# Linear attention and two mixers on one core: theta tiles loaded first, low parts and the first batch's products on VectorE, weight pieces at other units

## The chip, the cores and the metric

One core of a Trainium2 chip runs the whole program in one launch. The metric is the device time of an execution in microseconds. Three executions of the kernel before took 1168.22, 1164.98 and 1165.29 us; their median, 1165.29, is the time before. Engines are named as in the profile: PE (TensorE's matmuls; PEld its weight loads), DVE (VectorE), ACT (ScalarE), POOL (GpSimd), SP (SyncE, which here only issues transfers).

## What is computed

Eight batches of 576 tokens by 512 features go through three blocks. The reference, cut:

```python
kv = einsum('bhsd,bhse->bhde', k, v)      # attention without softmax, 8 heads of 64
x  = (q @ kv) / rms(q @ kv) * g_norm      # per head
theta = x @ w_theta
y = w_tok_r @ (x * cos(theta)) + w_tok_i @ (x * sin(theta))
u = x + y
x = u + relu(u @ w_ch)                    # first mixer
u = x + (relu(x.T @ w_tok1) @ w_tok2).T   # second mixer, over tokens: 576 -> 256 -> 576
out = u + relu(u @ w_ch1) @ w_ch2         # second mixer, over features: 512 -> 1536 -> 512
```

The weights come as float64 and are read as pairs of int32 words, from which the chip builds fp32 values.

## The kernel before, in words

**Products.** Every large product runs as three fp16 products, high by high, high by low and low by high (mm3, L82 to L84). So each operand needs a high part (an ACT copy to fp16) and a low part (value minus high part). "Decoding" a weight tile (L120 to L130) is one ACT instruction (L123) and three DVE instructions (L128, L129, L130). In `weight` (L132) the theta weights then take one ACT and one DVE instruction (L155, L157); all others take two ACT instructions (a scale, L150; the high part, L151) and one on POOL for the low part (L153).

**Units.** The work of a batch is cut into units: `attend` (normalised heads x, tiles a0 to a4), `rotate` (theta product pt, cosine and sine, multiply by x, high part zh and low part zl; r0 to r4), `mix` (M, products py over tokens, then uh and ul), `channel` (C, products pr, then xs high and low, and a DMA transpose of xs into xt, L464, after every second C unit), `token1` (H, products ph from xt, split at L71 and L72), `token2` (T, products pu; the result goes to a DRAM tile u2d). The two digits of M, C, H, T are the column chunk or part and the feature tile. In the first batch x reaches its transposed form by PE transposes (px, L322), later by DMA transposes (L330). `rotate_last` (L373) makes the last 64 tokens of both rotations as one tile zt (L399), which a DMA transpose (L400) puts into zh.

**Order.** `go` starts a unit after it has moved each pending unit on by one step (a yield). Lists of units (MIX, CHANNEL, STEADY) and a table, BESIDE, say what is started beside which unit: "a2", "r1" for the next batch, "l" for its loads, "n0" for the batch after that, "w" for a piece from the list `extra`. In the steady batches a piece is `stash` (L191): two transfers of 256 KB each on SP's queue at its start (wa_r or wb_r), seven steps later the decode (L128 to L130 on 128x512), sums on POOL (L213 to L216), the high part on ACT (L218), the low part on DVE (L220) and two stores. 24 such pieces prepare the weights of the last block and are spread over batches 1 to 6, five in a full batch. The program order that results goes through a scheduler, which may move an instruction ahead of others where its own simulation says so; urgent() puts the residual steps of `mix` and `channel` first.

**Transfers.** SP issues all loads of k, v, q and weights and all DMA transposes in one queue, in program order. POOL issues the stores to DRAM.

**Last block.** `mlp` (L545) handles 8 pairs of 288-column halves with seven products per 2x2 block. The first part forms pa, pb, pc (L555 on), the second na, nb, nc with the results added on DVE in `add` (L622). In program order the second part runs product 6 for both tiles, then 5, 7, 3, 4.

Of the kernel before, what the change touches and what calls it, by code (L numbers as in the profile page):

```python
# [28 lines left out]
def attn_mixer_kernel(  # L29
# [32 lines left out]
    def bank(name):  # L62
        return ps.tile([P, 512], F32, tag="ps", name=name)
# [68 lines left out]
    def weight(pool, w, src, part, n, hi, lo, scale, name, raw=None):  # L132

        val = pool.tile([P, S // 2], F32, tag="val", name=f"{name}v")[:part, :n] if pool is not stg else \
            pool.tile([P, n], F32, tag="val", name=f"{name}v")[:part]
        if w.dtype == F32:
            load(val, src)
            yield
        else:
            if raw is None:  # L140
                raw = pool.tile([P, 4, P, 2] if pool is not stg else [P, n, 2], I32, tag="raw", name=f"{name}r")
                if pool is not stg:
                    raw = raw.rearrange("p a n w -> p (a n) w")
                raw = raw[:part, :n]
                load(raw.rearrange("p n w -> p (n w)"), src)
            yield
            yield from decode(val, raw)
        if w is not w_theta:

            nc.scalar.activation(val, val, AF.Copy, scale=scale)  # L150
            nc.scalar.activation(hi, val, AF.Copy)  # L151
            yield
            nc.gpsimd.tensor_tensor(lo, val, hi, ALU.subtract)  # L153
            return
        nc.scalar.activation(hi, val, AF.Copy, scale=scale)  # L155
        yield
        nc.vector.scalar_tensor_tensor(lo, val, scale, hi, ALU.mult, ALU.subtract)  # L157
# [185 lines left out]
    def rotate(o, r):  # L343

        b = o.b
        if r == 0:
            prepare(o)
        zh, zl, x, xt = o.zh, o.zl, o.x[r], o.xt[r]
        if r == NR:
            yield from rotate_last(o, xt)  # L350
            return
        pt = bank(f"pt{b}{r}")
        mm3(pt, [(xt[:, 0, kk, :], xt[:, 1, kk, :], wth[:, kk, :], wtl[:, kk, :]) for kk in range(KD)])

        cs = fp.tile([P, 2, DM], F32, tag="cs", name=f"cs{b}{r}", bufs=2)
        f, sn = cs[:, 0], cs[:, 1]
        mul = nc.gpsimd if b == 0 else nc.vector
        yield
        nc.scalar.activation(f, pt, AF.Copy, bias=MAGIC)
        nc.vector.scalar_tensor_tensor(f, f, MAGIC, pt, ALU.subtract, ALU.subtract)  # L360
        yield
        nc.scalar.activation(sn, f, AF.Sin, scale=-RAD)
        nc.scalar.activation(f, f, AF.Abs)
        nc.scalar.activation(f, f, AF.Sin, bias=hpi, scale=-RAD)
        yield
        mul.tensor_tensor(cs, cs, x.unsqueeze(1).to_broadcast([P, 2, DM]), ALU.mult)
        yield
        at = slice(r, r + NR + 1, NR)
        nc.scalar.activation(zh[:, at, :], cs, AF.Copy)
        yield  # L370
        nc.vector.tensor_tensor(zl[:, at, :], cs, zh[:, at, :], ALU.subtract)  # L371
# [173 lines left out]
    def mlp(i, ck, following):  # L545
# [67 lines left out]
        def narrow(p, m, g, acc, first):  # L613
            ws, xs = PRODUCTS[p]
            h = hidden[g]
            part = (wb[0][:, g, m, ws], wb[1][:, g, m, ws], h.hi[:, xs], h.lo[:, xs])
            mm3(acc, [part], first=first and g == 0, last=g == KH - 1, skip_group_check=True)
# [30 lines left out]
            add(pb[m], m, 0, 0, True)  # L648
        nxt = next(following, None)

        def run(p, acc, first):
            for m in range(MH):
                if acc[m] is None:
                    acc[m] = bank(f"nc{i}{m}")[:, :NC]
                for g in range(KH):
                    narrow(p, m, g, acc[m], first)

        run(6, pa, False)
        for m in range(MH):
            add(pa[m], m, 0, 1)  # L660
        next(following, None)
        run(5, pc, True)
        for m in range(MH):
            add(pc[m], m, 1, 1)
        next(following, None)
        run(7, pa, False)
        for m in range(MH):
            add(pa[m], m, 1, 1, True)
        next(following, None)
        run(3, pc, False)  # L670
        for m in range(MH):
            add(pc[m], m, 0, 1, True)
        run(4, pa, False)
        for m in range(MH):
            add(pa[m], m, 1, 0, True)
        return nxt

# [28 lines left out]

    tk, cp, first = [], [], iter(())
    for j in range(KD):
        if j == 1:
            o = load_heads(0)  # L710
        go(weight_tile(stg, w_theta, wt, j, DM, ST / (2.0 * math.pi), "wt"))
    for part in range(2):
# [23 lines left out]
    def run(units, o, nxt, after, beside):  # L736
# [23 lines left out]
    TOKENS1 = ["K00", "H00", "H01", "K10", "H10", "H11"]  # L760
    STEADY = MIX[:6] + CHANNEL[:2] + MIX[6:] + CHANNEL[2:4] + ["K00"] + CHANNEL[4:] + TOKENS1[1:] + TOKEN2
    BESIDE = {
        "M00": "a2", "M01": "a3", "M02": "a4 l", "M03": "r0", "M10": "w", "M11": "r1", "M12": "r2", "M13": "w",
        "C03": "r4", "C11": "w", "H01": "r3", "H11": "n0 w", "T01": "n1", "T10": "w",
    }
    for b in range(B):
        loaded.clear()
# [23 lines left out]
        elif b == 1:  # L791
# [2 lines left out]
            run(MIX[4:6] + CHANNEL[:1], o, nxt, None, {"M10": "a2", "M11": "a3", "C00": "a4 l"})  # L794
            after = loaded[0]
            run(STEADY[STEADY.index("C01"):], o, nxt, after, {
                "C01": "r0", "M12": "r1", "M13": "r2", "C03": "r4", "C11": "w", "H01": "r3", "H11": "n0 w", "T01": "n1", "T10": "w",
            })
        elif b + 2 < B:
            at = STEADY.index("M02") + 1  # L800
# [81 lines left out]
```

## Time and profile before

| | |
|---|---|
| median of three executions | 1165.29 us |
| profiled execution, its own time | 1169.86 us |
| its span in the trace | 1168.1 us |
| PE busy | 1084.4 us, 93% |
| DVE busy | 823.4 us, 70% |
| ACT busy | 570.5 us, 49% |
| POOL busy | 266.8 us, 23%, nothing after about 600 us |
| mean granted clock of PE | 0.975 of full |

The span is what the profiler saw between first and last instruction; the execution's own time lies 1.8 us above it. The first batch takes the first 97 us and shares PE with the loading and decoding of the weights; batches 1 to 7 run until about 640 us, each some 73 to 78 us long; the last block fills the rest. "PEclk" is the granted clock as a share of 2.4 GHz: 1.00 is that level, and a stretch that reads between 0.5 and 1 was partly at 1.2 GHz.

### The profile page before, as it was taken

The numbers are of one execution on the slowest core, as the hardware profiler recorded it, in microseconds if no ns is written. First come the engines' busy times: TensorE is split into PE (matmuls) and PEld (weight loads), VectorE is DVE, ScalarE is ACT, GpSimd is POOL, SyncE is SP. The second block draws the span as 40 slices with busy tenths as digits, with TensorE's granted clock in tenths as the row PEclk, the third lists the DMA queues.
The fourth block names the chain that finished last, engine by engine and source line by source line (L and its number), as shares of the span: only waits on it lengthen the run. The fifth ranks groups of instructions, "written<-read, shape, count | busy, mean of one in ns | idle before, by whom it ended". The sixth has DMA issues, their size and how long they took to land.

```text
span 1168.1 us, 21694 instructions
## 1 busy us (share of the span) xinstructions
PE 1084.4 (93%) x8884; PEld 820.2 (70%) x8884; DVE 823.4 (70%) x1449; ACT 570.5 (49%) x980; POOL 266.8 (23%) x316
## 2 busy tenths in 40 slices
PE   4768889899998998999999999999999999999998
PEld 4456666576675875766677777777777777777776
DVE  3987857688787887787846395758567494848583
ACT  3766634646355454554724273626445362626261
POOL 2774134072542734625400000000000000000000
PEclk9879989999999998999999999999999999999999
DMA  9616446674766646745283801111010202010101
GB/s 319 210 69 142 104 124 147 167 185 107 215 148 173 184 124 176 184 127 145 59 246 78 308 2 42 41 36 47 23 60 11 72 11 72 1 57 26 37 6 41
DMA packets 146082, 126.34 MB, mean 108 GB/s; under 512 B 93184, under 2 KB 121984, under 8 KB 145984
## 3 DMA queue, kind: packets, MB, share of 16 engines
q1 hardware_dynamic: 140608, 104.53, 33.2%
q0 software_dynamic: 5376, 20.45, 5.0%
q8 instruction: 69, 1.13, 0.4%
q14 instruction: 29, 0.24, 0.1%
HBM read 74.29 MB, written 29.88 MB: 89 GB/s over the span
## 4 chain that ended last, share of the span: by engine, by line
PE 35%; DVE 28%; DMA 15%; ACT 10%; POOL 7%; issue 4%; SPq 1%; ACTq 0%; POOLq 0%; DVEq 0%
DMA xt<-xs 7%; PE na L82 3%; PE na L84 3%; PE na L83 3%; DVE gl L563 3%; DMA c<-u2d 2%; DVE gl L611 2%; POOL ri L308 2%; PE pa L82 2%; ACT gh L562 2%; PE pa L83 2%; PE pa L84 2%; DMA u2d<-R 1%; DVE zl L371 1%; PE nc L84 1%
## 5 line engine op out<-in xcount | busy, mean ns | idle before, releaser
L82 PE MATMUL py<-wmh,zh 128*128 128x256 f16 (+1 forms) x576 | 166.4, 289 | 9.4 <-DMA zh<-zt 6.0
L83 PE MATMUL py<-wml,zh 128*128 128x256 f16 (+1 forms) x576 | 166.3, 289 | 0.0
L84 PE MATMUL py<-wmh,zl 128*128 128x320 f16 (+1 forms) x512 | 146.1, 288 | 2.3 <-DVE zl L371 2.3
L82 PE MATMUL na<-gh,wbh 128*128 128x288 f16 x384 | 107.2, 287 | 9.8 <-DVE c L622 9.8
L83 PE MATMUL na<-gl,wbh 128*128 128x288 f16 x384 | 109.6, 288 | 0.0
L82 PE MATMUL pa<-o,wah 128*128 128x288 f16 x384 | 108.8, 286 | 0.9 <-DVE pre L605 0.9
L84 PE MATMUL na<-gh,wbl 128*128 128x288 f16 x384 | 109.5, 288 | 0.0
L83 PE MATMUL pa<-o,wah 128*128 128x288 f16 x384 | 109.5, 286 | 0.0
L84 PE MATMUL pa<-o,wal 128*128 128x288 f16 x384 | 108.7, 286 | 0.0
L622 DVE SCALAR_TENSOR_TENSOR c<-na,c 128x288 f32<-128x288 f32 x64 | 28.5, 455 | 81.2 <-PE na L84 81.2
L83 PEld LDWEIGHTS <-wbh 128*128 128x128 f16 x672 | 65.9, 98 | 27.6 <-issue 11.0
L563 DVE TENSOR_TENSOR gl<-sum,gh 128x1152 f16<-128x1152 f32 x48 | 65.1, 1356 | 24.3 <-ACT gh L562 23.5
L83 PEld LDWEIGHTS <-wah 128*128 128x128 f16 x672 | 65.8, 98 | 18.1 <-issue 1.3
L84 PEld LDWEIGHTS <-wbl 128*128 128x128 f16 x672 | 65.9, 98 | 16.8
L82 PEld LDWEIGHTS <-wbh 128*128 128x128 f16 x672 | 65.9, 98 | 16.8
L82 PEld LDWEIGHTS <-wah 128*128 128x128 f16 x672 | 65.8, 98 | 16.7
L84 PEld LDWEIGHTS <-wal 128*128 128x128 f16 x672 | 65.8, 98 | 16.6
L83 PE MATMUL pr<-ul,wch 128*128 128x256 f16 (+1 forms) x256 | 73.1, 286 | 3.4 <-DVE ul L430 3.4
L82 PEld LDWEIGHTS <-zh 128*128 128x128 f16 x576 | 57.1, 99 | 26.0 <-DMA zh<-zt 6.6
L82 PE MATMUL pr<-uh,wch 128*128 128x256 f16 (+1 forms) x256 | 73.0, 286 | 1.1 <-ACT uh L427 1.1
L84 PE MATMUL pr<-uh,wcl 128*128 128x256 f16 (+1 forms) x256 | 73.1, 286 | 0.0
L308 POOL TENSOR_TENSOR ri<-ss,mhalf 128x8 f32<-128x8 f32 x40 | 69.2, 1731 | 2.0
(311 smaller groups left out, 2983.9 us busy)
## 6 DMA issues: line engine op xcount, KB each, us to landing
q<-in_q SPq DMA_DIRECT2D x8, 1152.0 KB, 5.9
c<-u2d SPq DMA_DIRECT2D x32, 288.0 KB, 4.4
out<-c SPq DMA_DIRECT2D x64, 144.0 KB, 1.8
k<-in_k SPq DMA_DIRECT2D x24, 256.0 KB, 5.7
v<-in_v SPq DMA_DIRECT2D x24, 256.0 KB, 6.0
wa_r<-in_w_ch SPq DMA_DIRECT2D x24, 256.0 KB, 4.4
wb_r<-in_w_ch SPq DMA_DIRECT2D x24, 256.0 KB, 4.6
wad<-wa POOLq DMA_DIRECT2D x24, 224.0 KB, 2.4
```

The lines of the kernel that those rows point to most:

```text
L82: nc.tensor.matmul(acc, ah, bh, start=first and i == 0, stop=False, **more)
L83: nc.tensor.matmul(acc, ah, bl, start=False, stop=False, **more)
L84: nc.tensor.matmul(acc, al, bh, start=False, stop=last and i == n - 1, **more)
L308: nc.gpsimd.tensor_tensor(ri, ss, mhalf, ALU.pow)
L371: nc.vector.tensor_tensor(zl[:, at, :], cs, zh[:, at, :], ALU.subtract)
L562: nc.scalar.activation(h.hi[:, 3:], h.s, AF.Copy)
L563: nc.vector.tensor_tensor(h.lo[:, 3:], h.s, h.hi[:, 3:], ALU.subtract)
L611: nc.vector.tensor_tensor(h.lo[:, :3], h.own, h.hi[:, :3], ALU.subtract)
L622: nc.vector.scalar_tensor_tensor(dst, acc, 1.0 / SW**2, dst, ALU.mult, ALU.add)
```

## The change

1. Tiles 0 to 2 of the theta weights are loaded ahead of the first batch's k, v and q; before, only tile 0 was.
2. In the first batch the multiplication of cosine and sine by x (four instructions of 128x1024, L366) runs on DVE, not POOL.
3. All weights take the path that theta took: 22 low parts (9 token tiles of 576 columns, 4 channel tiles, 9 for the second mixer) go from POOL to DVE, and 22 scale instructions on ACT (L150) go away, the scale being part of the other two.
4. Pieces "w" start at M02, C10, H01, T01 and T12 where they started at M10, M13, C11, H11 and T10; in batch 1 at C10, H01, T01, T12 for C11, H11, T10.
5. The second part of `mlp` is written tile by tile: 5 and 6 of tile 0, 5 and 6 of tile 1, 7 and 3 of tile 0, 7 and 3 of tile 1, then 4.

Line numbers of the changed kernel are 7 to 10 lower behind `weight` (L464 is L456, L460 is L452, L399 is L391).

```diff
@@ weight
             yield
             yield from decode(val, raw)
-        if w is not w_theta:
-
-            nc.scalar.activation(val, val, AF.Copy, scale=scale)
-            nc.scalar.activation(hi, val, AF.Copy)
-            yield
-            nc.gpsimd.tensor_tensor(lo, val, hi, ALU.subtract)
-            return
         nc.scalar.activation(hi, val, AF.Copy, scale=scale)
         yield
         nc.vector.scalar_tensor_tensor(lo, val, scale, hi, ALU.mult, ALU.subtract)
@@ rotate
-        mul = nc.gpsimd if b == 0 else nc.vector
...
-        mul.tensor_tensor(cs, cs, x.unsqueeze(1).to_broadcast([P, 2, DM]), ALU.mult)
+        nc.vector.tensor_tensor(cs, cs, x.unsqueeze(1).to_broadcast([P, 2, DM]), ALU.mult)
@@ mlp
-        def run(p, acc, first):
-            for m in range(MH):
-                if acc[m] is None:
-                    acc[m] = bank(f"nc{i}{m}")[:, :NC]
-                for g in range(KH):
-                    narrow(p, m, g, acc[m], first)
-
-        run(6, pa, False)
+        def run(p, m, acc, first):
+            if acc[m] is None:
+                acc[m] = bank(f"nc{i}{m}")[:, :NC]
+            for g in range(KH):
+                narrow(p, m, g, acc[m], first)
+
+
         for m in range(MH):
+            run(5, m, pc, True)
+            add(pc[m], m, 1, 1)
+            run(6, m, pa, False)
             add(pa[m], m, 0, 1)
-        next(following, None)
-        run(5, pc, True)
+            next(following, None)
         for m in range(MH):
-            add(pc[m], m, 1, 1)
-        next(following, None)
-        run(7, pa, False)
+            run(7, m, pa, False)
+            add(pa[m], m, 1, 1, True)
+            run(3, m, pc, False)
+            add(pc[m], m, 0, 1, True)
+            if m == 0:
+                next(following, None)
         for m in range(MH):
-            add(pa[m], m, 1, 1, True)
-        next(following, None)
-        run(3, pc, False)
-        for m in range(MH):
-            add(pc[m], m, 0, 1, True)
-        run(4, pa, False)
-        for m in range(MH):
+            run(4, m, pa, False)
             add(pa[m], m, 1, 0, True)
         return nxt
@@ theta tiles and the first heads
     for j in range(KD):
-        if j == 1:
+        if j == KD - 1:
             o = load_heads(0)
         go(weight_tile(stg, w_theta, wt, j, DM, ST / (2.0 * math.pi), "wt"))
@@ steady batches; the table of batch 1 loses C11, H11, T10 and gains C10, H01, T01, T12 likewise
     BESIDE = {
-        "M00": "a2", "M01": "a3", "M02": "a4 l", "M03": "r0", "M10": "w", "M11": "r1", "M12": "r2", "M13": "w",
-        "C03": "r4", "C11": "w", "H01": "r3", "H11": "n0 w", "T01": "n1", "T10": "w",
+        "M00": "a2", "M01": "a3", "M02": "a4 l w", "M03": "r0", "M11": "r1", "M12": "r2",
+        "C03": "r4", "C10": "w", "H01": "r3 w", "H11": "n0", "T01": "n1 w", "T12": "w",
     }
```

**SP's queue at the end of `channel` in a steady batch (the fourth).** xt<-xs of 8x128 ends chunk 0, the two of 10x128 are chunk 1, zh<-zt is the next batch's last rotated tile, wa_r are halves of a piece. Before, from the transpose that ends chunk 0:

```order
L464 DMA_TRANSPOSE xt_2834<-xs_2972 128x8x128
L249 DMA k_3091<-in_k 96x512
L249 DMA v_3093<-in_v 96x512
L400 DMA_TRANSPOSE zh_2711<-zt_3058 128x8x128
L464 DMA_TRANSPOSE xt_3095<-xs_3096 128x10x128
L116 DMA wa_r<-in_w_ch 128x2x256
L464 DMA_TRANSPOSE xt_3095<-xs_3145 128x10x128
L116 DMA wa_r<-in_w_ch 128x2x256 x3
L249 DMA k_3563<-in_k 128x512
```

and in the changed kernel:

```order
L456 DMA_TRANSPOSE xt_2829<-xs_2963 128x8x128
L242 DMA k_3082<-in_k 96x512
L242 DMA v_3084<-in_v 96x512
L116 DMA wa_r<-in_w_ch 128x2x256 x2
L392 DMA_TRANSPOSE zh_2714<-zt_3050 128x8x128
L456 DMA_TRANSPOSE xt_3086<-xs_3087 128x10x128
L456 DMA_TRANSPOSE xt_3086<-xs_3128 128x10x128
L116 DMA wa_r<-in_w_ch 128x2x256 x4
L242 DMA k_3552<-in_k 128x512
```

The piece half that stood between the two transposes of chunk 1 is gone from there; two halves now stand ahead of zh<-zt, and four instead of three follow behind the last transpose.

**DVE at the same place.** R<-pr adds a channel product to the residual, xs<-R are the low parts that the transpose takes, wa_s is the decode of a piece. Before:

```order
L128 TENSOR_SCALAR wa_s<-wa_s 128x512
L452 SCALAR_TENSOR_TENSOR R_1648<-pr_3113,R_1648 128x320
L129 SCALAR_TENSOR_TENSOR wa_s<-wa_r,wa_s 128x512
L399 TENSOR_TENSOR zt_3058<-cs_3057,zt_3058 128x512
L460 SCALAR_TENSOR_TENSOR xs_3096<-R_1648,xs_3096 128x256
L460 SCALAR_TENSOR_TENSOR xs_3096<-R_1648,xs_3096 128x64
L130 SCALAR_TENSOR_TENSOR wa_s<-wa_r,wa_s 128x512
L452 SCALAR_TENSOR_TENSOR R_1648<-pr_3146,R_1648 128x320
L452 SCALAR_TENSOR_TENSOR R_1648<-pr_3165,R_1648 128x320
L460 SCALAR_TENSOR_TENSOR xs_3145<-R_1648,xs_3145 128x256
L460 SCALAR_TENSOR_TENSOR xs_3145<-R_1648,xs_3145 128x64
L460 SCALAR_TENSOR_TENSOR xs_3145<-R_1648,xs_3145 128x256
```

and in the changed kernel:

```order
L391 TENSOR_TENSOR zt_3050<-cs_3049,zt_3050 128x512
L444 SCALAR_TENSOR_TENSOR R_1626<-pr_3113,R_1626 128x320
L444 SCALAR_TENSOR_TENSOR R_1626<-pr_3129,R_1626 128x320
L452 SCALAR_TENSOR_TENSOR xs_3087<-R_1626,xs_3087 128x256
L452 SCALAR_TENSOR_TENSOR xs_3087<-R_1626,xs_3087 128x64
L452 SCALAR_TENSOR_TENSOR xs_3128<-R_1626,xs_3128 128x256
L452 SCALAR_TENSOR_TENSOR xs_3128<-R_1626,xs_3128 128x64
L444 SCALAR_TENSOR_TENSOR R_1626<-pr_3147,R_1626 128x320
L452 SCALAR_TENSOR_TENSOR xs_3128<-R_1626,xs_3128 128x256
L452 SCALAR_TENSOR_TENSOR xs_3128<-R_1626,xs_3128 128x64
L128 TENSOR_SCALAR wa_s<-wa_s 128x512
L129 SCALAR_TENSOR_TENSOR wa_s<-wa_r,wa_s 128x512
```

The three decode instructions that stood among the last R and xs steps follow behind the last xs; so the last four xs are no longer behind L130.

**DVE at the joint of two pairs of the last block.** c<-na, c<-nb and c<-nc are the additions of `add`; o, own and gl belong to the next pair's first part. Before:

```order
L622 SCALAR_TENSOR_TENSOR c_6785<-nb_7814,c_6785 128x288
L542 SCALAR_TENSOR_TENSOR o_7925<-t_7926,o_7924 128x1152
L585 TENSOR_TENSOR own_8160<-pb_8153,m_8151 128x288
L622 SCALAR_TENSOR_TENSOR c_6785<-nb_7818,c_6785 128x288
L610 TENSOR_TENSOR sum_7873<-own_7753,sum_7873 128x288
L563 TENSOR_TENSOR gl_7869<-sum_7873,gh_7868 128x1152
L585 TENSOR_TENSOR own_8194<-pb_8187,m_8177 128x288
L589 TENSOR_TENSOR own_8160<-pc_8196,u_8185 128x288
L622 SCALAR_TENSOR_TENSOR c_6785<-na_7806,c_6785 128x288
L622 SCALAR_TENSOR_TENSOR c_6785<-na_7810,c_6785 128x288
L622 SCALAR_TENSOR_TENSOR c_6785<-nc_7977,c_6785 128x288
L622 SCALAR_TENSOR_TENSOR c_6785<-nc_7996,c_6785 128x288
```

and in the changed kernel:

```order
L614 SCALAR_TENSOR_TENSOR c_6763<-nb_7792,c_6763 128x288
L534 SCALAR_TENSOR_TENSOR o_7903<-t_7904,o_7902 128x1152
L577 TENSOR_TENSOR own_8138<-pb_8131,m_8129 128x288
L614 SCALAR_TENSOR_TENSOR c_6763<-nb_7796,c_6763 128x288
L602 TENSOR_TENSOR sum_7851<-own_7731,sum_7851 128x288
L555 TENSOR_TENSOR gl_7847<-sum_7851,gh_7846 128x1152
L577 TENSOR_TENSOR own_8172<-pb_8165,m_8155 128x288
L581 TENSOR_TENSOR own_8138<-pc_8174,u_8163 128x288
L614 SCALAR_TENSOR_TENSOR c_6763<-nc_7909,c_6763 128x288
L614 SCALAR_TENSOR_TENSOR c_6763<-na_7784,c_6763 128x288
L614 SCALAR_TENSOR_TENSOR c_6763<-nc_7956,c_6763 128x288
L614 SCALAR_TENSOR_TENSOR c_6763<-na_7788,c_6763 128x288
```

Up to the last own both kernels have the same rows; of the four additions behind it, nc and na now alternate. Apart from the last pair, PE's queue differs by the same alternation alone: in both kernels it issues 15 matmuls of na directly behind the pb products that open the next pair.

## Rows read from the trace of the kernel before

**Rows 1.** Page, part 1: busy us, share of the span, instructions.

```profile
PE 1084.4 (93%) x8884; PEld 820.2 (70%) x8884; DVE 823.4 (70%) x1449; ACT 570.5 (49%) x980; POOL 266.8 (23%) x316
```

**Rows 2.** PE's waits over the whole span: total us, times, longest.

```profile
PE na L82 <- DVE c L622: 9.8, 6, 2.0
```

**Rows 3.** PE's waits, 0 to 97.4 us (the first batch).

```profile
PE px L322 <- DVE x L314: 7.2, 4, 3.1
...
PE py L82 <- ACT zh L369: 3.4, 1, 3.4
PE py L82 <- DMA zh<-zt: 3.0, 1, 3.0
```

**Rows 4.** PE's waits, 225 to 560 us (the steady batches).

```profile
PE ph L480 <- DMA xt<-xs: 15.7, 6, 4.2
PE pr L83 <- DVE ul L430: 3.0, 4, 0.9
```

**Rows 5.** Windows of token product 1 (ph): stretch, length, busy (instructions), PEclk, DMA share, GB/s.

```profile
295.00:302.83 7.83, 3.61 (x16) 0.00 (x0) 0.00 (x0) 1.00 1.04 270
...
sum 29.69, PE 25.47 DVE 1.64 ACT 2.37; mean PE 5.09 DVE 0.33 ACT 0.47
```

**Rows 6.** SP timeline, 366 to 375 us: start, us, instruction.

```profile
369.82 0.68 SPq L116 DMA_DIRECT2D wa_r<-in_w_ch  x1
370.63 1.33 SPq L464 DMA_TRANSPOSE xt<-xs  x1
```

**Rows 7.** DVE timeline, 364.3 to 371.2 us: start, us, instruction.

```profile
364.98 0.43 DVE L128 TENSOR_SCALAR wa_s<-wa_s 128x512 int32<-128x512 int32 x1
...
365.72 0.68 DVE L129 SCALAR_TENSOR_TENSOR wa_s<-wa_r,wa_s 128x512 int32<-128x512 int32 x1
...
367.40 0.68 DVE L130 SCALAR_TENSOR_TENSOR wa_s<-wa_r,wa_s 128x512 int32<-128x512 int32 x1
...
369.02 1.55 DVE L460 SCALAR_TENSOR_TENSOR xs<-R,xs 128x256 f16<-128x256 f32 x4
```

**Rows 8.** Chain that ended last: start, us to landing.

```profile
370.63 5.03 DMA xt<-xs
```

**Rows 9.** One line's instructions: transposes of xs issued by L464.

```profile
DMA to landing us min/median/max: 3.0/3.5/9.2
```

**Rows 10.** DVE by line and form, 230 to 600 us: busy, mean ns, idle before.

```profile
L371 DVE TENSOR_TENSOR zl<-cs,zh 128x1024 f16<-128x1024 f32 x21 | 26.9, 1283 | 4.5 <-ACT zh L369 4.3
L366 DVE TENSOR_TENSOR cs<-cs,x 128x1024 f32<-128x1024 f32 x20 | 25.5, 1275 | 6.0 <-ACT cs L364 5.9
```

**Rows 11.** DVE by line and form, 20 to 97 us.

```profile
L371 DVE TENSOR_TENSOR zl<-cs,zh 128x1024 f16<-128x1024 f32 x4 | 7.6, 1908 | 3.5 <-ACT zh L369 3.4
...
L157 DVE SCALAR_TENSOR_TENSOR wtl<-wt_3v,wth 128x512 f16<-128x512 f32 x1 | 0.7, 678 | 0.0
```

**Rows 12.** POOL by line and form, 16 to 97 us.

```profile
L309 POOL TENSOR_TENSOR x<-ri,gb 128x512 f32<-128x512 f32 x9 | 12.0, 1336 | 0.3
L366 POOL TENSOR_TENSOR cs<-cs,x 128x1024 f32<-128x1024 f32 x4 | 9.9, 2480 | 0.0
...
L153 POOL TENSOR_TENSOR wml<-wm_8v,wmh 128x576 f16<-128x576 f32 x1 | 2.3, 2257 | 0.0
...
L153 POOL TENSOR_TENSOR wcl<-wc_1v,wch 128x512 f16<-128x512 f32 x1 | 1.1, 1146 | 0.0
```

**Rows 13.** POOL timeline, 49 to 62 us.

```profile
53.82 2.87 POOL L366 TENSOR_TENSOR cs<-cs,x 128x1024 f32<-128x1024 f32 x1
```

**Rows 14.** DVE timeline, 49 to 62 us.

```profile
54.40 2.62 DVE L128 TENSOR_SCALAR wm_5v<-wm_5v 128x576 int32<-128x576 int32 x1
...
60.80 0.45 DVE L128 TENSOR_SCALAR wm_6v<-wm_6v 128x576 int32<-128x576 int32 x1
```

**Rows 15.** Windows, all engines: PE, PEld, DVE, ACT, POOL busy, PEclk, DMA share, GB/s.

```profile
0.00:20.00 20.00, 7.66 (x89) 6.90 (x90) 2.94 (x5) 2.95 (x4) 1.29 (x10) 1.00 0.88 278
...
97.40:163.00 65.60, 58.51 (x485) 40.30 (x483) 47.90 (x100) 40.96 (x87) 13.87 (x14) 0.93 0.55 134
```

More of the change, by code (lines that the diff above doesn't have):

```diff
@@ L796, in attn_mixer_kernel @@
             run(STEADY[STEADY.index("C01"):], o, nxt, after, {
-                "C01": "r0", "M12": "r1", "M13": "r2", "C03": "r4", "C11": "w", "H01": "r3", "H11": "n0 w", "T01": "n1", "T10": "w",
+                "C01": "r0", "M12": "r1", "M13": "r2", "C03": "r4", "C10": "w", "H01": "r3 w", "H11": "n0", "T01": "n1 w", "T12": "w",
             })
```

## The prediction

> **What bounds the kernel now.** I read the page's busy times first: PE is busy 1084.4 us, 93% of the span [rows 1], so a change that leaves the products alone can only win what PE waits, and the half clock that follows some waits. The view of PE's waits then says where. In the last block the largest item is 9.8 us for the additions on DVE [rows 2]. In the first batch PE waits for x out of DVE (7.2), for a high part zh (3.4) and for the DMA transpose of the last rotated tile (3.0) [rows 3]. In the steady batches nearly all of it is one thing: token product 1 (ph) waits six times, 15.7 us in all, for the DMA transpose xt<-xs, and a channel product waits 3.0 us for low parts ul [rows 4]. Third, windows of ph alone show what the waits cost beyond themselves: its 16 matmuls take 3.61 us where PE kept its full clock, and five such groups together 25.47 us [rows 5], so 25.47 - 5 x 3.61 = 7.4 us go to half clock behind the wait.
>
> Why that transpose is late is read from the two queues ahead of it. On DVE the three decode instructions of a weight piece (0.43, 0.68, 0.68 us) stand among the last residual and xs steps; the last four xs start at 369.02 and take 1.55 us, to 370.57 [rows 7]; the transpose is issued at 370.63 [rows 6]. So DVE sets the issue. SP sends a 256 KB half piece at 369.82 [rows 6], which is over by then and delays no issue, but it is in flight when the transpose starts: that one lands after 5.03 us [rows 8], against a median of 3.5 [rows 9].
>
> **Steady batches, the pieces moved.** The order shows the decode behind the last xs and the half piece gone from between the two transposes. Issue comes 0.43 + 0.68 + 0.68 = 1.8 us earlier, and landing another 5.03 - 3.5 = 1.5 earlier if nothing large is in flight. The mean wait is 15.7 / 6 = 2.6 us. Bounds: 1.8 off each wait, less where a wait is shorter, some 9 us; at best all 15.7. I take 12, since two half pieces now stand ahead of all three transposes and part of the 1.5 will not come. Of the 7.4 us at half clock I take 5 (0 to 7.4): it hangs on waits going, not shrinking. Of the 3.0 for ul, 2 (0 to 3.0), as a piece no longer starts beside M10 and M13. Against it: a piece's decode, POOL sums, high and low parts now run beside H, T and the next M units, where DVE had no piece before. No row shows that wait; the nearest is ul's, 3.0 us in four, 0.75 each [rows 4]. One per batch over four full batches is +3 (0 to +6). Behind a delayed DVE the next to be late would be R<-pu, and behind it POOL's store of u2d, which nobody needs until the last block. The k and v loads behind the four half pieces on SP start later; PE has a whole batch until it reads them, so 0. Sum -12 - 5 - 2 + 3 = **-16**, from -26 to -3.
>
> **First batch.** Added to DVE ahead of zt: four multiplications at 1.275 us [rows 10] = 5.1, nine low parts of 576 columns at 0.678 [rows 11] x 576/512 = 0.76, so 6.9, and two of 512, 1.4. Together 13.4. What goes is contention. A decode instruction that started at 54.40 took 2.62 us, where the same one at 60.80 took 0.45 [rows 14]; POOL was multiplying from 53.82 for 2.87 us, to 56.69 [rows 13]. Low parts zl took 1908 ns here [rows 11] and 1283 later [rows 10]. Adding up all DVE instructions from 20 to 97 us at the shortest duration of each shape gives 58.4 against 71.4, so 13.0 us were lost. POOL's large operations were 9.9 (multiplications), some 17.5 (eleven low parts of 1.1 to 2.3 us) and 12.0 (normalisation, L309) [rows 12]; the first two go, 27.4 of 39.4. I take 70% of 13.0, so 9 (0 to 13). Theta tiles 1 and 2 are decoded in the first 20 us, where DVE was busy 2.94 [rows 15]: 2 x (0.43 + 3 x 0.68) = 5 off the crowded part. Their loads, 0.52 MB each, stand ahead of k, v and q: at 278 GB/s [rows 15] at most 3.8 us, none if the transfers had room; I take 2. The multiplication itself is 2480 - 1275 = 1.2 us shorter [rows 10, 12], on the path of the last two tiles, for whose zh PE waited 3.4 [rows 3]: -2.4. Sum 13.4 - 9 - 5 + 2 - 2.4 = **-1**; with the bounds -7 to +10.
>
> **No effect.** The other eleven low parts (at most 0.7 us each, 7.5 in all) fall between 97 and 163 us, where DVE is busy 47.9 of 65.6 [rows 15]; idle DVE hides them, and without that cover they would cost what they take. The 22 scale steps leave ACT, on which no large wait ends. The last block: the rewrite changes the order of the text, but the queues differ only in that nc and na alternate; the na group that waits the 9.8 us still stands directly behind the next pair's opening products, with the same DVE rows ahead of its addition. So 0 (from -3 to +1, as products of nc now lie ahead of some of na).
>
> **Sum.** -16 - 1 = -17: 1169.86 - 17 = 1152.9 in terms of the profiled execution, which took 4.6 us more than the median of the three; against 1165.3 that is **1148 us**. A measurement of this kernel tells 0.3%, 3.5 us, from no change.
>
> **Rivals.**
> *DVE stays blocked in the first batch.* The nine L309 remain on POOL, and DVE now has more to run beside them. The decode at 54.40 ended at 57.02, 0.3 us behind POOL's operation: it was stopped, not slowed [rows 13, 14]. If each L309 (1336 ns, 12.0 in all) stops a DVE instruction for its length, relief is 1 us instead of 9, the first batch costs +7, and the time is 1156. For it: those two rows. Against it: L309 needs no DVE work beside it when it is itself the thing waited for. The Trainium skill's "SBUF — State Buffer" says it so, where the pair of ports that VectorE and GpSimd share is described: an exclusive lock for the whole instruction, the loser fully blocked, and an operation with two SBUF inputs is one that takes it; the moved multiplications and low parts are such operations, and the rows agree.
>
> *The transposes stay late.* Two half pieces (512 KB) now go out ahead of zh<-zt and both xt<-xs, where one stood between them. If these transfers, not DVE's issue, set the landing, the waits and the half clock stay; left are 1 from the first batch and some 3 of ul: 1161 (1158 to 1166). For it: 5.03 us with one half piece in flight [rows 6, 8]. Against it: the issue itself comes 1.8 us earlier, whatever the queue holds. The Trainium skill's "DMA: Bandwidth & Descriptors" (on HWDGE ordering) states that each DMA engine takes the descriptors of a ring in order; by it all three transposes would queue behind both halves. No row of the kernel before shows two halves directly ahead.
>
> *DVE becomes the bound of the first stage*, and the kernel is slower. With no relief, theta's decode not hidden and the loads at their upper bound, the path to zt grows by 13.4 + 3.8 = 17 us, and PE, waiting in more places, loses some 4 more to the half clock, as behind ph [rows 5]. That is +21 against -16, so 1170. It decides from the point where the first batch costs more than the 16 that the steady batches give. Against it: the contended rows are what POOL's departing work made.
>
> *Everything goes*: no wait for xt, full clock, no new wait, first batch at its lower bound: -26 - 7 = -33, so 1132.
>
> That the change does not do what it says is true of the last block, and is in the forecast.
>
> **How the numbers follow.** Forecast 0.58 (own range 1140 to 1157), blocked DVE 0.13, late transposes 0.13, DVE as bound 0.07, everything 0.09. Faster by over 0.3% (under 1161.8): the forecast, blocked DVE, everything and 0.06 of the late transposes, 0.86. Within: the rest of these and 0.01 of the bound, 0.08. Slower 0.06. The range 1137 to 1161 leaves out the bound, half of the late transposes and half of the last case, 0.18.
>
> **What would show it.** Right: PE's waits for xt<-xs at ph under 5 us in all; PEclk near 1.00 in the windows of ph; the last transpose issued within 0.1 us of the last xs, and about 1.8 us earlier against PE's channel products; PE waiting for zh<-zt of the first batch no longer than the 3.0 of now; decode instructions of 576 columns near 0.45 us there. The row of 9.8 us for L622 unchanged. Wrong: xt<-xs landing after 5 us and more with PE still waiting; or the first batch over 10 us longer; or a new PE wait of over 5 us for hh, R or k and v; or the na wait gone.

## The result, and the profile after

The changed kernel takes 1158.12 us (median of 4, 1156.94 to 1159.02) against 1166.76 (median of 4) for the kernel before, measured beside it. The medians are 8.6 us apart; the ratio of the comparison, 0.9913 with a 95% interval of 0.989 to 0.9937, stands for 10 us, and the two traces differ by 10.8. The forecast was 17 us less. The time lies in the range of 1137 to 1161, but not for the reasons given: the stretch that was to win 16 us won nothing, and the one that was to win 1 won most of the gain. That the number still fell into the range is luck.

Where the time went shows when both traces are cut at the same places of the program (first matmul of a product of a batch). The windows of the changed kernel: length, busy us of PE, PEld, DVE, ACT and POOL, PEclk, DMA share, GB/s.

```profile
0.00:54.00 54.00, 31.99 (x237) 22.99 (x238) 38.16 (x59) 28.26 (x46) 18.11 (x25) 0.87 0.74 260
54.00:110.50 56.50, 48.15 (x371) 34.94 (x372) 50.56 (x83) 36.55 (x66) 19.09 (x15) 0.88 0.52 135
110.50:156.00 45.50, 41.17 (x382) 29.94 (x380) 32.69 (x80) 22.50 (x49) 0.00 (x0) 0.92 0.53 133
156.00:225.90 69.90, 66.08 (x555) 47.38 (x554) 54.94 (x94) 34.56 (x62) 26.64 (x34) 0.98 0.59 153
225.90:528.60 302.70, 286.71 (x2418) 206.91 (x2416) 235.81 (x413) 154.81 (x276) 138.72 (x189) 0.97 0.64 162
528.60:585.50 56.90, 54.41 (x434) 39.98 (x432) 43.20 (x76) 31.08 (x56) 20.26 (x25) 0.97 0.39 86
585.50:647.60 62.10, 62.10 (x466) 45.38 (x464) 30.86 (x68) 15.92 (x27) 1.49 (x3) 1.00 0.61 182
647.60:1157.30 509.70, 495.73 (x4034) 394.32 (x4031) 339.17 (x611) 236.51 (x378) 1.38 (x2) 1.00 0.13 45
```

| stretch, by PE's products | before | changed | difference |
|---|---|---|---|
| start to py of batch 0 | 56.3 | 54.0 | -2.3 |
| to pr of batch 0 | 59.8 | 56.5 | -3.3 |
| to pu of batch 0 | 49.5 | 45.5 | -4.0 |
| to py of batch 2 | 72.5 | 69.9 | -2.6 |
| four steady batches, to py of batch 6 | 303.0 | 302.7 | -0.3 |
| batch 6 | 53.6 | 56.9 | +3.3 |
| batch 7 | 62.1 | 62.1 | 0 |
| last block | 511.2 | 509.7 | -1.5 |

Batches 6 and 7 are shorter than the 73 to 78 us that were given for all of batches 1 to 7: 53.6 and 62.1 us before.

Each trace shows a single execution. Seven traces of this case (the kernel before and the runs below that leave its table of pieces alone) took 301.9 to 305.5 us for the four steady batches, so a difference of some 3 us there is not told from the spread between executions.

PE's waits from 225 to 560 us, where before xt<-xs had 15.7 and ul 3.0 [rows 4]:

```profile
PE pr L82 <- ACT uh L419: 8.5, 4, 3.1
PE pr L83 <- DVE ul L422: 5.1, 4, 1.3
PE ph L472 <- DMA xt<-xs: 2.0, 3, 1.2
```

The wait that the change was to remove is down to 2.0 us, and PE waits 13.6 us for uh and ul at the channel products instead. The half clock moved with the wait. Below are the four steady batches, first with the instructions on pr alone, then with those on ph alone, each time before and changed: length, busy us of PE (number of matmuls), then of DVE and ACT, and PEclk, DMA share and GB/s of the whole stretch.

```profile
238.10:541.10 303.00, 50.00 (x384) 13.75 (x32) 0.98 0.62 161
225.90:528.60 302.70, 57.99 (x384) 14.22 (x32) 0.97 0.64 162
238.10:541.10 303.00, 31.38 (x112) 5.44 (x8) 4.63 (x8) 0.98 0.62 161
225.90:528.60 302.70, 25.53 (x112) 5.49 (x8) 4.65 (x8) 0.97 0.64 162
```

The same matmuls of ph take 5.9 us less, those of pr 8.0 us more. So the steady batches are no shorter. One of the four places, in the fourth batch, shows what the new wait is: ACT, then DVE (start, us, instruction, idle time before it and what ended it).

```profile
344.69 0.95 ACT L211 ACTIVATE wa<-wa_s 128x896 f16<-128x896 f32 x1 [2.33 <-POOL wa_s L209]
345.55 0.58 ACT L351 ACTIVATE cs<-pt 128x512 f32<-128x512 f32 x1
347.40 0.63 ACT L354 ACTIVATE cs<-cs 128x512 f32<-128x512 f32 x1 [1.27 <-DVE cs L352]
...
348.72 0.72 ACT L356 ACTIVATE cs<-cs,hpi 128x512 f32<-128x512 f32 x1
349.35 0.45 ACT L419 ACTIVATE uh<-R 128x320 f16<-128x320 f32 x1
```

```profile
345.68 1.09 DVE L213 SCALAR_TENSOR_TENSOR wa<-wa_s,wa 128x896 f16<-128x896 f32 x1 [1.87 <-ACT wa L211]
...
347.28 0.48 DVE L418 TENSOR_TENSOR R<-py,R 128x320 f32<-128x320 f32 x1
349.48 1.23 DVE L358 TENSOR_TENSOR cs<-cs,x 128x1024 f32<-128x1024 f32 x1 [1.71 <-ACT cs L356]
```

ACT stood 2.33 us for POOL's last sum of the piece that now starts at M02 before it could make its high part (L211); DVE stood 1.87 for that and made the low part (L213); only then came R<-py of the last M product at 347.28, and its uh stood behind three steps of a rotation until 349.35.

In the first 97.4 us [rows 3]; the first line is of the kernel before, the others of the changed one:

```profile
PE po L294 <- DVE x L314: 3.4, 1, 3.4
...
PE px L315 <- DVE x L307: 7.1, 3, 2.8
PE py L84 <- DVE zl L363: 3.2, 2, 1.8
PE py L82 <- ACT zh L361: 2.7, 2, 2.2
...
PE py L82 <- DMA zh<-zt: 0.9, 1, 0.9
```

The wait for x at po (the products q by kv) is gone, that for the last rotated tile fell from 3.0 to 0.9, and that for the low parts zl rose from 1.5 to 3.2. DVE's instructions on the rotated tiles run at their undisturbed length there, zl at 1216 ns against 1908 [rows 11]:

```profile
L363 DVE TENSOR_TENSOR zl<-cs,zh 128x1024 f16<-128x1024 f32 x4 | 4.9, 1216 | 0.0
...
L358 DVE TENSOR_TENSOR cs<-cs,x 128x1024 f32<-128x1024 f32 x4 | 4.9, 1216 | 0.2 <-ACT cs L356 0.2
```

The last block waits as before [rows 2]:

```profile
PE na L82 <- DVE c L614: 9.3, 6, 1.9
```

### The profile page after: what moved, and what is told of

Read it like the earlier page. It is cut to its first block, busy times and chain, and to the rows that moved or that the text cites. A ratio compares the mean times of both kernels' runs of the same rounds, so it can differ in the third digit from the quotient of the medians.

```text
span 1157.3 us, 21691 instructions
## 1 busy us (share of the span) xinstructions
PE 1086.3 (94%) x8884; PEld 821.8 (71%) x8884; DVE 825.4 (71%) x1475; ACT 560.2 (48%) x958; POOL 225.7 (20%) x290
## 4 chain that ended last, share of the span: by engine, by line
PE 37%; DVE 30%; DMA 13%; ACT 9%; POOL 6%; issue 4%; SPq 1%; POOLq 0%; ACTq 0%; DVEq 0%
DMA xt<-xs 3%; PE na L82 3%; PE na L84 3%; PE na L83 3%; DVE gl L555 3%; DVE gl L603 3%; DVE cs L358 3%; DMA c<-u2d 2%; DMA u2d<-R 2%; PE pa L82 2%; ACT gh L554 2%; PE pa L83 2%; PE pa L84 2%; PE nc L84 1%; PE nc L82 1%
## 5 line engine op out<-in xcount | busy, mean ns | idle before, releaser
L82 PE MATMUL pr<-uh,wch 128*128 128x256 f16 (+1 forms) x256 | 77.1, 302 | 11.0 <-ACT uh L419 11.0
L555 DVE TENSOR_TENSOR gl<-sum,gh 128x1152 f16<-128x1152 f32 x48 | 65.0, 1354 | 24.3 <-ACT gh L554 23.5
L83 PE MATMUL pr<-ul,wch 128*128 128x256 f16 (+1 forms) x256 | 77.3, 302 | 5.1 <-DVE ul L422 5.1
L82 PEld LDWEIGHTS <-wah 128*128 128x128 f16 x672 | 65.7, 98 | 16.6
L84 PEld LDWEIGHTS <-wbl 128*128 128x128 f16 x672 | 65.7, 98 | 16.6
L82 PEld LDWEIGHTS <-wbh 128*128 128x128 f16 x672 | 65.7, 98 | 16.6
L84 PEld LDWEIGHTS <-wal 128*128 128x128 f16 x672 | 65.7, 98 | 16.6
L84 PE MATMUL pr<-uh,wcl 128*128 128x256 f16 (+1 forms) x256 | 77.1, 301 | 0.0
L82 PEld LDWEIGHTS <-zh 128*128 128x128 f16 x576 | 56.9, 99 | 21.1 <-ACT zh L361 3.4
```

The lines of the kernel that those rows point to most:

```text
L82: nc.tensor.matmul(acc, ah, bh, start=first and i == 0, stop=False, **more)
L83: nc.tensor.matmul(acc, ah, bl, start=False, stop=False, **more)
L84: nc.tensor.matmul(acc, al, bh, start=False, stop=last and i == n - 1, **more)
L555: nc.vector.tensor_tensor(h.lo[:, 3:], h.s, h.hi[:, 3:], ALU.subtract)
```

## The experiments

All ratios are to the kernel before, measured beside each run on the same chip, with 95% intervals. The edits are named by the numbered parts of the change: theta loads (1), multiplications (2), low parts (3), tables of pieces (4), last block (5). "pu at" is the time at which the first batch's token product 2 starts; it was 165.6 before.

### The parts alone

**Tables alone** (`"M02": "a4 l w"`, `"C10": "w"` and so on in the kernel before).

> The kernel before with part 4 alone (pieces at M02, C10, H01, T01, T12). In the trace of the changed kernel PE waits 13.7 us less for xt<-xs, but 9.9 us more for uh and ul, and four steady periods take 302.7 us against 303.0. Theory S (the gain is made in the first batch, the moved pieces only move the wait): about 3 us less than the kernel before, ratio 0.997 (0.994 to 1.001), with waits of PE for uh and ul over 10 us and for xt<-xs under 4. Rival T (the prediction: the moved pieces are worth 16 us, and something of the other parts eats it): ratio 0.986 (0.983 to 0.991), with uh and ul as in the kernel before, 4.5 us.

Measured 1.0007 (0.999 to 1.0024). PE's waits in its four steady batches:

```profile
PE pr L82 <- ACT uh L427: 6.6, 4, 1.9
PE pr L83 <- DVE ul L430: 5.3, 4, 1.3
PE ph L480 <- DMA xt<-xs: 4.2, 4, 1.5
```

Theory S holds, but for a wait at xt of 4.2 where it asked for under 4; T falls: uh and ul 11.9, no time won. This run also shows what the change did to batch 6, which is 56.8 us long here, as in the changed kernel, with the same wait for uh:

```profile
PE pr L82 <- ACT uh L427: 2.2, 1, 2.2
536.10:592.90 56.80, 54.61 (x435) 39.98 (x433) 43.26 (x76) 31.10 (x56) 20.27 (x25) 0.97 0.39 90
```

So the 3 us lost in batch 6 are the moved pieces' as well.

**Multiplications and low parts on DVE.**

> The kernel before with parts 2 and 3 alone (the first batch's multiplications and all low parts on DVE, no scale step on ACT; theta loads and tables as before). Theory S: most of the 10 us that the changed kernel is ahead when the first batch's token product pu starts comes from here: ratio 0.993 (0.990 to 0.996), pu of the first batch at about 157 us against 165.6. Rival T: DVE takes what POOL gave, ratio 1.000 (0.997 to 1.005), pu at 164 to 168.

Measured 0.9972 (0.9956 to 0.9988), pu at 160.5. The ratio lies in T's range, pu between the two; the gain is less than half of what S asked.

**Theta tiles first.**

```diff
-        if j == 1:
+        if j == KD - 1:
```

> The kernel before with part 1 alone (theta tiles 0 to 2 ahead of k, v, q). The first products po start later, in the changed kernel by 1 to 3 us, and DVE has 5 us of decode less behind them. Theory S: the late start and the freed DVE nearly cancel, ratio 1.000 (0.997 to 1.002). Rival T, by the prediction's terms (+2 for the loads, -5 for the decode): ratio 0.997 (0.995 to 0.999).

Measured 1.0026 (1.001 to 1.0042): slower by 3 us, outside both ranges. The first po starts at 19.9 instead of 17.9, the first py at 59.4 instead of 56.3, so the later loads are not made up for by the 5 us of decode that DVE is spared. Further on the one trace does not keep this delay (py of batch 2 at 238.5 against 238.1), so where the 3 us stay is not shown.

**Second part of the last block tile by tile.**

> The kernel before with part 5 alone (second part tile by tile in the text). The queues differ only in how na and nc alternate. Both theories: ratio 1.000 (0.998 to 1.002), PE's wait for c at na 9 to 10 us as before. A third one, that the last block's 1.5 us less in the trace of the changed kernel is this part's: ratio 0.9985, and a span from the first pa to the end of 509.7 instead of 511.2 us.

Measured 1.0005 (0.9991 to 1.002): nothing. The 1.5 us of the last block above are not this part's: seven traces with it, the changed kernel's among them, took 509.7 to 511.5 us there, and seven without it 509.2 to 511.2.

The parts alone add up to about 0.1% slower, 1.0007 + 0.9972 + 1.0026 + 1.0005 - 3 = 1.001; together they win 0.87%. So they need each other, and the next runs show where.

**Parts 1, 2 and 3 together.**

> The kernel before with parts 1, 2 and 3 (all of the first batch's parts, tables and last block as before). Part 1 alone cost 0.26%, parts 2 and 3 alone won 0.28%. Theory J (they need each other: DVE can only take POOL's work when theta's decode is out of its way): ratio 0.992 (0.989 to 0.995), the first batch's pu at 155 to 158 us. Rival A (effects add up): ratio 1.000 (0.998 to 1.002), pu at about 163.

Measured 0.9940 (0.9928 to 0.9952), pu at 156.7: theory J. The effects do not add up: theta first costs 3 us alone, and is worth 0.3% on top of the work moved to DVE. Of the changed kernel's gain this is 7 of 10 us; the interval of the whole change, 0.989 to 0.9937, overlaps with this one, so the other 3 us are not told from nothing.

**Parts 1 and 2** (low parts left on POOL).

> The kernel before with parts 1 and 2 (theta first, multiplications on DVE; the low parts stay on POOL). Theory J1 (the multiplications are what delays zh, 2.5 us each on POOL behind its low parts): ratio 0.995 (0.992 to 0.998). Theory J2 (POOL's low parts are what delays the normalisation and the DVE): ratio 1.000 (0.998 to 1.003).

Measured 0.9940 (0.9927 to 0.9952), the same as with the low parts on DVE: J1, and a little more gain than its middle value. Moving the 22 low parts is worth nothing once the multiplications are gone from POOL. The time that DVE loses beside POOL can be counted by adding up its instructions from 20 to 97 us and taking off the shortest duration of each shape: 13.9 us were lost before, 13.3 in this run, 5.2 with parts 1 to 3 and 4.9 in the changed kernel. From this run to parts 1 to 3 the loss fell by 8.1 us, but the eleven low parts that came to DVE there (nine at 0.75, two at 0.68) are 8.1 us of work: DVE is busy 67.5 us here and 67.4 there. So equal times do not tell whether the loss mattered.

**Part 2 alone** (four multiplications).

```diff
-        mul = nc.gpsimd if b == 0 else nc.vector
...
-        mul.tensor_tensor(cs, cs, ...
+        nc.vector.tensor_tensor(cs, cs, ...
```

> The kernel before with part 2 alone (multiplications of the first batch on DVE). Parts 1 and 2 together won 0.6%, with part 3 on top no more; part 1 alone lost 0.26%. Theory M (the multiplications carry the gain by themselves; theta first costs its 2 to 3 us unless DVE is short): ratio 0.995 (0.993 to 0.997). Theory J (they need theta's decode out of the way): ratio 0.999 (0.997 to 1.001).

Measured 0.9956 (0.994 to 0.9971): theory M. PE's waits up to 97.4 us for zh and for x at po, 3.4 each before:

```profile
PE py L82 <- ACT zh L368: 2.8, 1, 2.8
PE po L294 <- DVE x L314: 2.0, 1, 2.0
```

Four instructions carry 5 us. From the first py to the first pr this trace is 4.3 us shorter than the one before (59.8 to 55.5). Of PE's waits in that stretch x at po lost 1.4, zh 0.6, the DMA transpose zh<-zt 1.8 (3.0 to 1.2), v and kvbd together 1.3, which is 5.1 in all; PE is busy 0.7 us longer. With theta first as well it is 7 (the intervals overlap); with the low parts but without theta first only 3.3 (0.9972): that DVE is then short, and that this is where theta's early decode counts, fits these numbers but was not tested by itself.

### The wait that moved

**Piece of M02 at M10.**

```diff
-        "M00": "a2", "M01": "a3", "M02": "a4 l w", "M03": "r0", "M11": "r1", ...
+        "M00": "a2", "M01": "a3", "M02": "a4 l", "M03": "r0", "M10": "w", "M11": "r1", ...
```

> The changed kernel with the piece of M02 started at M10 instead (as the kernel before has one there). On ACT its high part then stands behind the uh of M13, on DVE its low part behind the last R<-py; in the changed kernel both stand ahead and wait for POOL's sums. Theory W (these two instructions are the new wait): PE's waits for uh and ul from 230 us on fall from 16 to about 5 us, xt<-xs stays under 5, and the half clock behind the wait goes: about 1147 us, ratio to the kernel before 0.982 (0.978 to 0.987). Rival Q (the wait for uh is the rotations' own chain on ACT and DVE, the piece only shares it): uh and ul stay over 11 us, ratio 0.991 (0.988 to 0.994).

Measured 0.9894 (0.9875 to 0.9912). uh and ul fell to 4.8 us as W said, and by that Q falls; but ph waited again, 15.9 us in the four batches where W had under 5, and the gain of 0.9% over the changed kernel that W promised did not come. The ratio is one that Q had asked for.

**Piece of M02 at M12.**

> The changed kernel with the piece of M02 started at M12 instead. Its high and low parts then come behind the last uh and ul, but its decode stands among the last xs on DVE, as in the kernel before. Theory W: uh and ul fall to about 5 us from 230 us on, and PE waits for xt<-xs again, 8 to 12 us with half clock behind it: ratio 0.990 (0.987 to 0.994). Rival Q: uh and ul stay over 11 us and xt<-xs comes on top, ratio 0.997 or more.

Measured 0.9881 (0.9866 to 0.9896), the shortest of all (1152.44 us), though its interval overlaps that of the run with the piece at M10 and, just, that of the changed kernel. The waits are as W expected, in its four steady batches:

```profile
PE ph L472 <- DMA xt<-xs: 9.7, 4, 3.6
PE pr L83 <- DVE ul L422: 3.5, 4, 1.3
PE pr L82 <- ACT uh L419: 0.6, 1, 0.6
```

These two runs show what the high and low part did, and that there is a second wait behind the first. DVE adds the last channel product 2.8 to 2.9 us after PE finished it before, and in three of four batches with the piece at M12. In the changed kernel this lag is 0 to 0.3 us in three of four batches; there PE had stood still for uh and ul shortly before. Batch 6 is back at 54.9 (M10) and 53.8 us (M12).

**Piece of M02 at T03**, and **pieces at C10, H01, T01, T10, T13**, to take pieces off DVE from M12 to the last xs.

> The changed kernel with the piece of M02 started at T03 instead, so that no piece's decode, high or low part stands on DVE between the fourth M unit's neighbours and the last xs of a steady batch (from M12 to C13). In the kernel before and with the piece at M12, DVE adds the last channel product 2.8 to 2.9 us after PE has finished it, and xt<-xs comes late by that; in the changed kernel the lag is gone only because PE stood still for uh. Theory D (DVE's backlog in this stretch is what PE waits for, at uh, ul or xt as the order has it): the lag falls under 1 us, PE waits from 230 to 520 us fall to under 7 us in all, about 1140 us, ratio to the kernel before 0.977 (0.971 to 0.984). Rival L (the way through xs and the DMA transpose is too long by itself): the lag falls, PE still waits 2 us and more per batch for xt<-xs, ratio 0.988 (0.985 to 0.991).

> The changed kernel with steady pieces at C10, H01, T01, T10, T13: another order that has no piece between M12 and the last xs, with the spread over T different. Theory D: within 0.3% of the run with T03, lag under 1 us. Rival L: ratio 0.988 (0.985 to 0.991).

Measured 0.9942 (0.9919 to 0.9965) and 0.9896 (0.9872 to 0.992). Both missed D's numbers (the second ratio lies in L's range), and neither tests it over all four batches: only batch 2 was free of the piece. In batches 3 to 5 DVE had the low part of a piece between R<-py of M12 and of M13 as in the changed kernel, since a piece that starts later pushes the next ones on. The T03 run then waited up to 5.6 us for uh. Batch 2, free of the piece, still waited 2.6 and 2.7 us for uh and ul and was 75.6 and 75.2 us long, against 75.9 in the changed kernel and 74.3 before: without the piece, part of that wait remains.

**Pieces at C10, H01, T00, T02, T10 and rotations r1, r2 at M10, M11.**

```diff
-        "M02": "a4 l w", "M03": "r0", "M11": "r1", "M12": "r2", ... "C10": "w", "H01": "r3 w", "T01": "n1 w", "T12": "w",
+        "M02": "a4 l", "M03": "r0", "M10": "r1", "M11": "r2", ... "C10": "w", "H01": "r3 w", "T00": "w", "T01": "n1", "T02": "w", "T10": "w",
```

> The changed kernel with steady rotations r1 and r2 started at M10 and M11 (not M11 and M12) and pieces at C10, H01, T00, T02, T10. In the runs with T03 and with T10, T13 the piece had come back between M12 and M13 in batches 3 to 5, so they did not test theory D. Here, in batches 2 to 5, DVE's queue has neither a piece's instruction nor a rotation's multiplication between the R<-py of M12 and that of M13, and no decode up to the last xs. Theory D (what stands on DVE ahead of the last R<-py and the last xs is what PE waits for): lag of the last R behind pr under 1 us, PE's waits for uh, ul and xt<-xs from 230 to 520 us under 6 us in all, ratio to the kernel before 0.977 (0.971 to 0.984). Rival L (the way through xs and the transpose is too long by itself, or the wait moves again): 2 us and more of waiting per batch at one of them, ratio 0.988 (0.985 to 0.992).

Measured 0.9886 (0.9866 to 0.9907): rival L. From M12 to the last xs nothing of a piece is left on DVE, the waits for uh and ul are nearly gone, and PE waits almost as long as before, now for xt:

```profile
PE ph L472 <- DMA xt<-xs: 14.5, 6, 4.1
PE pr L82 <- ACT uh L419: 0.5, 1, 0.5
PE pr L83 <- DVE ul L422: 0.2, 1, 0.2
```

In the fifth batch PE ended its last channel product at 428.10. DVE and ACT then hand the work to and fro: residual on DVE, high part on ACT, low parts on DVE, then the next residual, 1.50 us each round. DVE:

```profile
428.86 0.48 DVE L444 SCALAR_TENSOR_TENSOR R<-pr,R 128x320 f32<-128x320 f32 x1
429.88 0.56 DVE L452 SCALAR_TENSOR_TENSOR xs<-R,xs 128x256 f16<-128x256 f32 x2 [0.54 <-ACT xs L445]
430.36 0.48 DVE L444 SCALAR_TENSOR_TENSOR R<-pr,R 128x320 f32<-128x320 f32 x1
431.38 0.56 DVE L452 SCALAR_TENSOR_TENSOR xs<-R,xs 128x256 f16<-128x256 f32 x2 [0.54 <-ACT xs L445]
431.85 0.48 DVE L444 SCALAR_TENSOR_TENSOR R<-pr,R 128x320 f32<-128x320 f32 x1
432.87 0.56 DVE L452 SCALAR_TENSOR_TENSOR xs<-R,xs 128x256 f16<-128x256 f32 x2 [0.54 <-ACT xs L445]
```

ACT:

```profile
430.88 0.47 ACT L445 ACTIVATE xs<-R 128x320 f16<-128x320 f32 x1 [1.03 <-DVE R L444]
432.37 0.47 ACT L445 ACTIVATE xs<-R 128x320 f16<-128x320 f32 x1 [1.03 <-DVE R L444]
```

DVE stands 0.54 us for ACT and ACT 1.03 us for DVE in each round. The last residual starts at 431.85, the transpose goes out at 433.73, and PE goes on at 438.89:

```profile
438.89 0.58 PE L472 MATMUL ph<-xt,w1h 128*128 128x512 f16 x1 [3.91 <-DMA xt<-xs]
```

PE's waits ahead of pr and ph (gaps from 0.05 us up), added over batches 2 to 5 of each trace, with the lag of the last residual behind the last channel product:

| kernel | for uh, ul | at ph | sum | lag in the four batches | four batches |
|---|---|---|---|---|---|
| before | 3.8 | 12.8 | 16.6 | 2.9, 2.9, 2.9, 2.9 | 303.0 |
| parts 1 to 3 | 3.8 | 12.9 | 16.7 | 2.9, 2.9, 2.9, 2.9 | 302.9 |
| tables alone | 11.9 | 4.3 | 16.2 | 2.4, 0.7, 0.7, 2.4 | 300.7 |
| changed | 13.6 | 2.1 | 15.7 | 0.0, 0.0, 2.4, 0.3 | 302.7 |
| piece at M10 | 4.8 | 15.9 | 20.7 | 4.2, 4.2, 3.7, 4.2 | 304.1 |
| piece at M12 | 4.1 | 9.7 | 13.8 | 1.1, 2.8, 2.8, 2.8 | 296.8 |
| piece at T03 | 15.9 | 0.8 | 16.7 | 0.0, 0.0, 0.7, 0.7 | 305.4 |
| T10 and T13 | 12.2 | 3.5 | 15.7 | 0.0, 0.0, 2.4, 2.4 | 301.0 |
| last run | 0.8 | 14.5 | 15.3 | 3.1, 4.1, 3.8, 3.9 | 302.0 |

Nine kernels with seven tables of pieces: the sum is 14 to 17 us in eight of them and 20.7 with the piece at M10. A kernel that waits less ahead of pr mostly waits more at ph. Where a row is shorter than its sum would say, PE had more of its full clock: it is busy 283.0 us with the piece at M12 and 286.7 in the changed kernel and in the last run. The 296.8 us of M12 come from the fastest of that kernel's five executions (1147.93, median 1152.44), the 304.1 us of M10 from the slowest of its six.

Why the sum stays is not shown. The last run's rows suggest a relay between DVE, ACT and the transpose that is longer than the work PE has meanwhile. Its length is not fixed: from the last M product to the matmul of ph that follows the last transpose, a batch took 21.4 to 23.6 us before, 22.8 to 25.5 in the changed kernel and 21.0 to 24.3 in the last run. No run shortened the relay itself (other buffers for xs, the high part on DVE). One rival is untested: in the changed kernel two residuals stand together on DVE ahead of four low parts, while in the last run and with the piece at M10 residuals and low parts alternate, and these two have the longest lags, 3.1 to 4.2 us. Their wait for xt may be that order's.

## Why the prediction was right and wrong

**The number.** 1158.12 us lies in the range of 1137 to 1161, but 1 us outside the 1140 to 1157 that the forecast gave for its own case, and in the range of the rival with late transposes (1158 to 1166), which had the wait for xt stay; it went. The first batch made up for what the steady batches did not give.

**Steady batches, -16: wrong.** Its first half came true. The transpose no longer waits behind a decode, xt<-xs fell by 13.7 us (12 forecast), and the windows of ph run at full clock, 3.6 us for 16 matmuls (5 us forecast; PE's busy time in ph fell by 5.9). The step that failed is the give-back, +3 with a bound of +6, priced by the wait for ul at 0.75 each. The waits for uh and ul rose by 9.9 us, above the bound, and ul, forecast at -2, is +2.1 of that. With them came a term that was put at nothing: half clock at pr, 8.0 us more of PE's busy time. Together the four batches ran at PEclk 0.97 against 0.98 before, PE busy 286.7 against 284.9:

```profile
238.10:541.10 303.00, 284.89 (x2419) 205.97 (x2417) 237.65 (x413) 154.77 (x276) 143.05 (x189) 0.98 0.62 161
```

Behind it is a wrong reading: I took the decode among the xs for the cause of the late transpose and its removal for a gain, and did not ask whether the next thing in line on the same two engines was just as late. In the last run, with no piece in that stretch, the lag is 3.1 to 4.1 us.

Of the 1.5 us for landing about half came. The transpose that took 5.03 [rows 8] takes 4.83 with no half piece between the two, but over the four batches the last transpose landed after 4.1 us on average, against 4.8 before.

```profile
361.71 4.83 DMA xt<-xs
```

The signs that were to show the forecast right nearly all came: xt under 5 (2.0), full clock at ph, zh<-zt no longer than 3.0 (0.9), the wait at na as before. Only the last transpose was issued 0.2 to 0.8 us behind the last xs, not 0.1. One sign for wrong, a new wait of over 5 us, came too, but at uh, which was not on its list. The signs looked at the place of the old wait; the stretch as a whole would have shown that nothing was won.

**First batch, -1: right sign, size wrong.** Parts 1 to 3 measured -7 us. The relief was sized well (9 forecast, 13.9 - 4.9 = 9.0 measured; the forecast's own count of what was lost, 13.0, comes out as 13.9 when it is redone). Whether relief and added work belong in the sum one for one is not shown: DVE is busy 65.5 us from 20 to 97 us before and 67.4 with parts 1 to 3, and yet the time is 7 us less, so it does not follow DVE's busy time alone. The multiplications were sized at -2.4 beside 5.1 of work for DVE; alone they measured -5. The -2.4 was to come off the wait for zh, which fell by only 0.6; the rest came from x at po, zh<-zt and the smaller waits named above. Theta first was sized -5 + 2 = -3; alone it measured +3, and beside the multiplications some -2 (0.9956 to 0.9940, with intervals that overlap).

**No effect: half right.** The last block stayed (9.3 us for 9.8, part 5 alone 1.0005). The stretch behind the first batch did not: to pu it is 4.0 us shorter in the trace. The wait for zh<-zt there fell from 3.0 to 0.7, but the run of parts 1 to 3 is as short there, 45.9 us, with 2.3 of that wait left, so this wait is not the cause. In the run without part 3 that stretch won only 1 us in its trace; the timing shows no gain of part 3.

**Batch 1 and batch 6** were not in the sum. Batch 1 lost its wait of 2.9 for xt, but the stretch of 69.9 us lies only 0.6 below the 70.5 to 72.5 of the seven traces with the table of before. Batch 6 is 3.3 us longer, with a wait of 2.5 for uh and PEclk 0.97; tables alone show the same, and it is back at 53.8 and 54.9 us where the piece left M02 for M12 and M10.

**Rivals.** DVE did not stay blocked by the nine L309: the time it lost beside POOL fell from 13.9 to 4.9 us as POOL's busy time from 20 to 97 us fell from 57.6 to 35.9. By the exclusive lock that the Trainium skill's "SBUF — State Buffer" (section "SBUF: two separate sides") describes, that loss should shrink with POOL's work, and here it did. The transposes did not stay late behind the two half pieces: of the two at the end of a steady batch the first landed after 4.5 us on average (3.5 before), the last after 4.1 (4.8 before), and the wait for them went. DVE did not become the bound, though parts 2 and 3 without part 1 (0.9972) are behind part 2 alone (0.9956, the intervals overlap), which leans that way. The rival that came true was not on the list: the removed wait comes back at the next place.

## What to carry to other kernels

When one wait is removed from a chain in which two engines hand work to and fro, ask what the same engines do next, and whether that would be just as late: then the wait only moves, and the half clock with it. Add up waits and busy time over the whole stretch before and after, not one row, and choose signs of success that do so too. An engine's busy time is not by itself a cost: DVE's rose from 65.5 to 67.4 us in the first batch while the time fell by 7 us, and four multiplications moved off POOL were worth 5.

## What was not expected of the hardware

A DVE decode instruction with a single operand in SBUF took 2.62 us beside a POOL multiplication and 0.45 without [rows 13, 14], and with POOL's multiplications and low parts gone most of the time that DVE lost beside POOL went (13.9 to 4.9 us). The transposes' landing, median 3.5 us [rows 9], stayed at 3.4 to 3.5 in the changed kernel, with the piece at M12 and in the last run, wherever the pieces' transfers stood in the queue; the last transpose of a steady batch, the one PE waits for, is slower than that median, 4.8 us before and 4.1 in the changed kernel on average.
